# Gradient tail of an attention and MLP kernel: b2's sums and one addend of dx moved from products to VectorE, dx rows in two parts, other buffers

## The chip, the cores and the metric

The kernel runs on one core of a Trainium2 chip. A core has five engines, each with its own in-order queue: TensorE (PE, matrix products into PSUM; its weight loads are the row PEld), VectorE (DVE), ScalarE (ACT), GpSimd (POOL) and SyncE (SP, which here only issues transfers). Transfers issued by SP and POOL run on the core's 16 DMA engines. The metric is the device time of one execution in microseconds; a profile of one more execution shows what each engine did.

## The reference, cut to what matters

The forward function normalizes x, runs 32-head attention s on it, runs a gated MLP on it that has a second layer norm, and returns x + s * silu(MLP). What is computed is that output (out_0) and the gradients of a given grad_out for x, wqkv, wo, w1, b1, w2 and b2 (out_1 to out_7).

```python
xn = _layernorm(x, axis=-1)
s = _A_ref(xn, A_wqkv, A_wo)                     # softmax attention, H = 32, then @ wo
# _B_ref: y = _layernorm(xn); h = gelu(y @ w1 + b1); m = h @ w2 + b2
g = _silu(_B_ref(xn, B_w1, B_b1, B_w2, B_b2))
return x + s * g
# reference: _out, _vjp = jax.vjp(_f, A_x, A_wqkv, A_wo, B_w1, B_b1, B_w2, B_b2)
#            returns (_out, *_vjp(grad_out))
```

Sizes: S = 2048 rows, D = 512 columns, F = 1792 hidden units; all inputs and outputs bf16.

## The kernel before, in words

Rows are worked in NT = 16 tiles of 128, D in IC = 4 blocks of 128, F in FC = 14. Three parts follow each other. `Pre` normalizes, projects and runs the MLP forward (0 to about 220 us). `attention_core` runs the attention forward and backward for all heads (to about 1862 us). `Grads` computes the rest: its `tail_open` and `tail_mid` are called at the end of the attention loop, its `run` after it. The instructions of each engine run in the order in which the code emits them, and a step waits for the data and buffers that it needs; nothing reorders them. So the order of the code, the number of buffers in a ring, and the order of SP's transfers set the time.

The stages of `Grads.run`, with the lines that matter:

- **Rows of the output (so).** For each row tile t, `emit_oT` transposes the attention output (L575, copied by ScalarE, L577) and `emit_so` multiplies with wo (L584). VectorE makes two tiles from that product: dm (L586, kept in `dm_all`) and t1 (L588, float32, in the ring "t13" of two buffers). POOL adds x to t1 (L597) and stores two rows at a time (L599, out_0). `load_s1` (L526) loads the operands, two row tiles at a time, into four buffers; the two last lie in `s1w`, whose columns 12 to 15 of 16 are free. `emit_dmT` transposes dm (L719, L720) and, for b2's gradient, which is the sum of dm over all rows, multiplies it with a column of ones (L721), 16 products into one PSUM bank of its own (`psdb2`). From t = 12 on, dwo (L732) is mixed in.
- **dw2** (L742): 14 groups of 16 products. Each needs a transposed load of the hidden layer (`load_hg`, L711, four buffers). VectorE and ScalarE meanwhile compute the slope of gelu in 49 steps (`slope_step`, L667 to L688).
- **dwq, dwkv** (L822, L830): 12 groups of 16 products. SP's queue here holds, in this order of the loop index i: transposed loads of dKV (L793), of w2 (L790, two for each i from 4 to 10), of y (L860), and of w1 (L863, one for each i from 8 to 11).
- **dh and dy** by groups of four row tiles: `emit_dh` (L878) multiplies with w2T, VectorE multiplies each product with the slope and sums it for b1 (L881); the result goes out through transposes (L885, L886). `emit_dy` (L912) multiplies with w1T, and `ln_a` (L901 to L905) does the backward of a layer norm: ScalarE sums the row (L901), VectorE multiplies and sums (L902), combines (L904) and makes the bias (L905); ScalarE scales the row (L915, into `dxm_all`).
- **dw1** (L984): per four hidden blocks (`ci`) two passes of 32 products, over pieces that SP loads (L950) into five buffers; evictions in `evac` (ScalarE L727, VectorE L725), stores by POOL and SP (L993) from three output buffers.
- **dx rows** (L1013 to L1025), between the third and the fourth dw1: 13 products for each row tile, the first of them the identity times `dxm_all` (L1013), the share of the second layer norm; then `ln_a` on the PSUM result, ScalarE's scaling (L1020), the addition of grad_out on POOL (L1022, on VectorE for the two last), and the store (L1025). Operands come in groups of four row tiles by `load_dx` (L1003 to L1005).

The product tiles come from the PSUM ring `psA` (five banks), transposes from `psT` (two), and `psS` holds `psdb2`.

Of the kernel before, what the change touches and what calls it, by code (L numbers as in the profile page):

```python
# [489 lines left out]
class Grads:  # L490
# [88 lines left out]
    def emit_so(self, t):  # L579
        nc = self.nc  # L580
        oT = self.oTs.pop(t)
        ps = self.pA([128, D], f32, "ps_so")
        for cc in range(IC):
            nc.tensor.matmul(ps[:], lhsT=oT[:, cc, :], rhs=self.wo_sb[:, cc, :], start=(cc == 0), stop=(cc == IC - 1))  # L584
        g, x = self.s1[t // 2]
        nc.vector.tensor_tensor(out=self.dm_all[:, t, :], in0=ps[:], in1=g[:, t % 2, 1, :], op=ALU.mult)  # L586
        t1 = self.row("t13")
        nc.vector.tensor_tensor(out=t1[:], in0=ps[:], in1=g[:, t % 2, 0, :], op=ALU.mult)  # L588
        self.flush_adds()
        self.adds.append((t, t1, x))  # L590

    def flush_adds(self):
        nc = self.nc
        for t, t1, x in self.adds:
            if t % 2 == 0:
                self.ot = self.row("ot")
            nc.gpsimd.tensor_tensor(out=self.ot[:, t % 2, :], in0=t1[:], in1=x[:, t % 2, :], op=ALU.add)  # L597
# [12 lines left out]
    def run(self):  # L610
        nc, k, tc, ctx = self.nc, self.k, self.tc, self.ctx
        out_2, out_3, out_4, out_5, out_6, out_7 = self.outs[2:]
        slots = ctx.enter_context(tc.tile_pool(name="p3_slots", bufs=1, reuse_waits="tile"))
        psA = ctx.enter_context(tc.tile_pool(name="p3_psA", bufs=5, space=PSUM, reuse_waits="tile"))
        psS = ctx.enter_context(tc.tile_pool(name="p3_psS", bufs=1, space=PSUM, reuse_waits="tile"))
        psT = ctx.enter_context(tc.tile_pool(name="p3_psT", bufs=2, space=PSUM, reuse_waits="tile"))
        self.pT = lambda shape, dt, name: psT.tile(shape, dt, name=name, tag="tp")
        self.pA = lambda shape, dt, name: psA.tile(shape, dt, name=name, tag="mm")
# [14 lines left out]
        db1acc = slot("db1acc", [128, FC, 4], "db1acc", f32)  # L633
        db1f = slot("db1f", [128, FC], "db1f", f32)
        lns = [slot(f"lns{i}", [128, 4], f"lns{i}", f32) for i in range(4)]
        ones_bf = slot("ones", [128, 1], "ones_bf")
        db2 = slot("db2", [1, D], "db2")
        slot("pad", [128, 32], "pad_to_256g")
        self.s1w = slot("w2T", [128, NT, D], "s1w")
        sl = slot("sl", [128, 5, 4, 512], "sl")  # L640
# [70 lines left out]
            tr(out=hgr[:, fc % 4], in_=k.HGT_s[fc * 128:fc * 128 + 128, :])  # L711

        dmT, dm_all = self.dmT, self.dm_all
        psdb2 = psS.tile([1, D], f32, name="psdb2")

        def emit_dmT(t):
            pt = self.pT([128, IC, 128], bf16, "dm_tp")
            for b in range(IC):
                nc.tensor.transpose(pt[:, b, :], dm_all[:, t, b * 128:(b + 1) * 128], k.ident_bf[:])  # L719
            nc.scalar.copy(out=dmT[:, :, t * 128:(t + 1) * 128], in_=pt[:])  # L720
            nc.tensor.matmul(psdb2[0:1, :], lhsT=ones_bf[:, 0:1], rhs=dm_all[:, t, :], start=(t == 0), stop=(t == NT - 1))  # L721

        def evac(out, in_, e):
            if e:
# [25 lines left out]
        self.load_s1(3)  # L750
        self.load_s1(4)
        ld(out=dso_all[:, 0:8], in_=dsov[:, 0:8])
        nc.vector.memset(ones_bf[:], 1.0)

        nd = 0
        for t in range(2, NT):
# [22 lines left out]
        while nd < NT:  # L779
            emit_dmT(nd)  # L780
            nd += 1
        nc.vector.tensor_copy(out=db2[:], in_=psdb2[0:1, :])
        st(out=out_7.rearrange("(o d) -> o d", o=1), in_=db2[:])

        xn1 = slot("xg", [128, NT, D], "xn1")
        dKVn = [self.pO.tile([128, NT, 4, 128], bf16, name="dKVn0", tag="Oall")]
# [54 lines left out]
        for i in range(12):  # L841
            part, ic = i // 4, i % 4
            if part == 0:
                emit_dwq(ic)
            else:
                emit_dwkv(ic, part - 1)
            if i == 0:
                load_dkv(0, 3)
            if i < 3:
                load_h1(3, 1 + i)  # L850
            if 1 <= i <= 4:
                load_dkv(1, i - 1)
            if 4 <= i <= 10:
                for _ in range(2):
                    if nw < FC:
                        load_w2T(nw)
                        nw += 1
            if i == 7:
                y_all = self.pO.tile([128, NT, D], bf16, name="y_all", tag="Oall")
                ld(out=y_all[:], in_=k.Y_s.rearrange("(t p) d -> p t d", p=128))  # L860
            if i >= 8:
                j = i - 8
                tr(out=w1T[:, :, j, :], in_=self.B_w1[j * 128:j * 128 + 128, :])  # L863
            slope_step(1 + i % 2)


# [90 lines left out]
        for h4 in range(4):  # L957
            tr(out=dQT[:, 4 * h4:4 * h4 + 4].rearrange("c t b s -> c (t b) s"),
               in_=k.dQall[:, 4 * h4:4 * h4 + 4, :].rearrange("s t c -> s (t c)"))
        dy_group(2)  # L960
        R = [self.early.tile([128, 4, S], bf16, name="R0", tag="dmT"), None]
        rv = k.dKVT_s.rearrange("(r p) s -> p r s", p=128)
        dy_group(3)
        R[1] = slot("xg", [128, 4, S], "R1")
        xn_all = self.pO.tile([128, NT, D], bf16, name="xn_all", tag="dQall")
        dor = slot("hgw", [128, 3, 4, D], "dor")
        r2r = slot("gp1", [128, 4, D], "r2r", f32)
        dxr = slot("gp2", [128, 8, D], "dxr")
        nc.vector.reduce_sum(out=db1f[:], in_=db1acc[:], axis=AX.X)

# [2 lines left out]
        def emit_dw1(ci):  # L973
            c0, cn = CH[ci]
            w = cn * 128
            for ih in range(2):
                pss = [self.pA([128, 512], f32, "ps_dw1") for _ in range(2)]
                for tg in range(4):
                    pc = pieces[(ci, tg)]
                    for t4 in range(4):  # L980
                        t = tg * 4 + t4
                        for i2 in range(2):
                            ic = ih * 2 + i2
                            nc.tensor.matmul(pss[i2][:, 0:w], lhsT=y_all[:, t, ic * 128:(ic + 1) * 128], rhs=pc[:, 0:cn, t4, :],  # L984
                                             start=(t == 0), stop=(t == NT - 1))
                    if ih == 1 and nx[0] < 16:
                        pieces[order[nx[0]]] = load_piece(*order[nx[0]])
                        nx[0] += 1
                for i2 in range(2):
                    ic = ih * 2 + i2  # L990
                    ob = ob_tile()
                    evac(ob[:, 0:w], pss[i2][:, 0:w], i2)
                    (st if i2 and ci < 3 else ld)(out=out_4[ic * 128:(ic + 1) * 128, c0 * 128:c0 * 128 + w], in_=ob[:, 0:w])  # L993

        emit_dw1(0)
        psb = self.pT([FC, 128], f32, "db_tp")
        nc.tensor.transpose(psb[:], db1f[:], k.ident_f[:])
        db1 = slot("db2", [FC, 128], "db1")
# [9 lines left out]
        load_dx(0)  # L1008
        emit_dw1(2)
        load_dx(1)  # L1010
        for t in range(NT):
            ps = self.pA([128, D], f32, "ps_dxa")
            nc.tensor.matmul(ps[:], lhsT=k.ident_bf[:], rhs=dxm_all[:, t, :], start=True, stop=False)  # L1013
            for cc in range(IC):
                nc.tensor.matmul(ps[:], lhsT=dQT[:, t, cc, :], rhs=wT[:, cc, :, :], start=False, stop=False)
            for rc in range(8):
                nc.tensor.matmul(ps[:], lhsT=R[rc // 4][:, rc % 4, t * 128:(t + 1) * 128], rhs=wT[:, 4 + rc, :, :], start=False, stop=(rc == 7))
            r, nb = ln_a(ps[:], xn_all[:, t, :], k.rstd1[:, t:t + 1])
            r2 = r2r[:, t % 4, :]
            nc.scalar.activation(out=r2, in_=r[:], func=ACT.Identity, bias=nb, scale=k.rstd1[:, t:t + 1])  # L1020
            dx = dxr[:, t % 8, :]
# [1 line left out]
            if t in (1, 5):  # L1023
                load_dx(2 + t // 4)
            ld(out=self.o1[t * 128:(t + 1) * 128, :], in_=dx)  # L1025
        emit_dw1(3)


# [489 lines left out]
```

## Time and profile before

| what | us |
|---|---|
| median of 3 runs | 2208.2 (2205.89 to 2212.59) |
| profiled execution | 2206.27 |
| its span, first to last instruction | 2204.4 |
| PE busy in the span | 2147.6 (97%) |
| DVE busy | 1899.9 (86%) |
| ACT busy | 1758.4 (80%) |
| POOL busy | 590.3 (27%) |
| TensorE clock granted, mean | 0.998 |

The page and the trace give, for each line of the code, the busy time of its instructions, the idle time of the engine before them and what ended that idle time ("<- DVE dm_all L586"). A group is named by line, engine, operation and by what it writes and reads. Times in a timeline are from the start of the span. A busy PE is not a PE at its peak, and the idle time of an engine that nobody waits for costs nothing. Where an instruction waits for several things, the profile names the one that came last by its own record, which can be another than the true one.

### The profile page before, as it was taken

Reading aid. Unit: us, or ns where it says so; the run is one execution under the profiler, and the core shown is the slowest. Engines: PE = TensorE matmul, PEld = TensorE weight load, DVE = VectorE, ACT = ScalarE, POOL = GpSimd, SP = SyncE. Lnnn points to the kernel's source line nnn. Section 1 sums busy time; section 2 is a strip of 40 time slices with the busy share of each in tenths; the row PEclk is TensorE's granted clock in tenths of the full one; section 3 lists DMA queues with packets and bytes.
Section 4 is the critical chain, followed back from the end, with each engine's and each line's share of the span. In section 5 each row is a group of like instructions: output and inputs, shape, how many; then the busy total and the mean of one; then the engine's idle time right before and its main releaser. Section 6 shows DMA issues by size and latency. Waiting matters only on the chain.

```text
span 2204.4 us, 74272 instructions
## 1 busy us (share of the span) xinstructions
PE 2147.6 (97%) x30690; PEld 1192.5 (54%) x30690; DVE 1899.9 (86%) x3696; ACT 1758.4 (80%) x2481; POOL 590.3 (27%) x1373
## 2 busy tenths in 40 slices
PE   6999999999999999999999999999999999999998
PEld 3444555555555555555555555555555555444444
DVE  6677899999999999999999999999999998798624
ACT  5764888888888888988888989888888887784214
POOL 4276222122223222221312222222222132510002
PEclk9999999999999999999999999999999999999999
DMA  7786999999999999999999999999999999999974
GB/s 236 244 276 201 214 190 202 198 196 204 202 194 197 205 199 198 200 199 203 199 199 203 199 196 206 191 205 198 193 212 200 197 209 210 296 262 234 246 200 154
DMA packets 1422066, 461.14 MB, mean 209 GB/s; under 512 B 1334622, under 2 KB 1405918, under 8 KB 1421728
## 3 DMA queue, kind: packets, MB, share of 16 engines
q1 hardware_dynamic: 1407424, 425.46, 101.6%
q0 software_dynamic: 12720, 29.37, 4.9%
q8 instruction: 240, 3.93, 0.8%
q10 hardware_dynamic: 1584, 1.57, 0.2%
q14 instruction: 98, 0.80, 0.1%
HBM read 62.79 MB, written 64.75 MB: 58 GB/s over the span
## 4 chain that ended last, share of the span: by engine, by line
PE 90%; DVE 4%; issue 2%; ACT 2%; DMA 2%; POOL 1%; SPq 0%; DVEq 0%; ACTq 0%; POOLq 0%
PE tT L1194 24%; PE d L1115 15%; PE X L1229 10%; PE Z L1332 10%; PE X L1232 5%; PE X L1236 5%; PE ps_dw L742 2%; PE ps_dy L912 2%; PE ps_dw L984 2%; PE ps_h L352 2%; PE s L1093 2%; PE ps_m L367 2%; PE ps_dh L878 2%; PE tT L1264 1%; PE ps_dwkv L830 1%
## 5 line engine op out<-in xcount | busy, mean ns | idle before, releaser
L1133 DVE TENSOR_TENSOR gts<-d,ets 128x512 bf16<-128x512 f32 x2048 | 1366.4, 683 | 110.4 <-ACT ek L1211 46.7
L1102 ACT ACTIVATE ets<-s 128x1024 bf16<-128x1024 f32 x1024 | 1047.8, 1023 | 170.1 <-PE s L1093 82.2
L1194 PEld LDWEIGHTS <-ets 128*128 128x128 bf16 x6790 | 429.4, 97 | 248.3 <-issue 245.6
L1194 PE MATMUL tT<-ident_bf,ets 128*128 128x128 bf16 x6790 | 545.9, 219 | 14.2 <-ACT ek L1211 2.1
L1211 ACT COPY ek<-tT 128x448 f32<-128x448 f32 (+2 forms) x1024 | 510.4, 498 | 4.0 <-DVE ek L1211 1.3
L1115 PE MATMUL d<-QDT,KVT 32*128 32x512 bf16 x2048 | 450.0, 385 | 0.0
L1093 PE MATMUL s<-QDT,KVT 32*128 32x512 bf16 x2048 | 400.6, 381 | 2.6 <-ACT ets L1102 2.6
L1115 PEld LDWEIGHTS <-KVT 32*128 32x128 bf16 x2048 | 130.1, 91 | 319.2 <-issue 319.2
L1229 PE MATMUL X<-ets,NAT 128*32 128x256 bf16 x4096 | 300.5, 284 | 0.3 <-DVE xs L1245 0.3
L1236 PE MATMUL X<-gts,NAT 128*17 128x256 bf16 x4096 | 289.5, 273 | 0.0
L1232 PE MATMUL X<-ets,Lc 128*32 128x256 bf16 x4096 | 289.5, 273 | 0.0
L1392 POOL COPY tick<-gts 1x2 bf16<-1x2 bf16 x205 | 35.8, 174 | 629.7 <-DVE gts L1133 629.7
L1332 PE MATMUL Z<-gk,W 128*32 128x512 bf16 x2048 | 197.8, 379 | 1.1 <-DVE acc L1346 1.1
L1332 PE MATMUL Z<-ek,W 128*32 128x512 bf16 x1792 | 198.4, 379 | 0.0
L1229 PEld LDWEIGHTS <-NAT 128*32 128x32 bf16 x4096 | 105.9, 93 | 114.8 <-issue 21.9
L1293 POOL TENSOR_TENSOR W<-NATQq,rL 128x128 bf16<-128x128 bf16 x64 | 25.3, 396 | 503.4 <-DVE rL L1292 391.2
L1093 PEld LDWEIGHTS <-KVT 32*128 32x128 bf16 x2048 | 123.6, 91 | 8.5 <-issue 6.1
L1332 PEld LDWEIGHTS <-W 128*32 128x32 bf16 x4096 | 113.8, 97 | 11.7 <-issue 1.7
L1232 PEld LDWEIGHTS <-Lc 128*32 128x32 bf16 x4096 | 107.9, 96 | 0.0
L1236 PEld LDWEIGHTS <-NAT 128*17 128x17 bf16 x4096 | 103.4, 92 | 3.1
L1332 PE MATMUL Z<-ekd,W 128*32 128x512 bf16 x256 | 97.0, 379 | 0.0
L1197 PE MATMUL tT<-ident_bf,ets 128*128 128x128 bf16 x378 | 82.8, 219 | 0.0
(252 smaller groups left out, 2493.9 us busy)
## 6 DMA issues: line engine op xcount, KB each, us to landing
gk<-gts SPq DMA_TRANSPOSE x512, 5.3
H1T_s<-h1r SPq DMA_DIRECT2D x28, 256.0 KB, 3.9
HGT_s<-hgT SPq DMA_DIRECT2D x8, 896.0 KB, 4.4
DH_s<-stg SPq DMA_DIRECT2D x12, 512.0 KB, 3.2
hch<-DH_s SPq DMA_DIRECT2D x12, 512.0 KB, 4.4
gp<-H1T_s SPq DMA_DIRECT2D x9, 512.0 KB, 7.5
out_dram<-ob_w POOLq DMA_DIRECT2D x36, 128.0 KB, 4.6
NAT_s<-NS SPq DMA_DIRECT2D x4, 1056.0 KB, 6.2
```

The costliest lines, as they stand in the source:

```text
L352: nc.tensor.matmul(ps[:], lhsT=w1_sb[:, ic, fc * 128:(fc + 1) * 128], rhs=yT[:, ic, g * 512:(g + 1) * 512], start=(ic == 0), stop=(ic == I ...
L1093: nc.tensor.matmul(s[:, hj, :], lhsT=op["KVT"][r:r + 32, kb * 128:(kb + 1) * 128], rhs=op["QDT"][r:r + 32, qc * 512:(qc + 1) * 512], start ...
L1102: nc.scalar.activation(out=st_et[g][:, :, :, a[1] % 4, :].rearrange("k b h q -> k h b q"), in_=cur["s"][:].rearrange("k h (b q) -> k h b q ...
L1115: nc.tensor.matmul(d[:], lhsT=op["KVT"][r:r + 32, kb * 128:(kb + 1) * 128], rhs=op["QDT"][r:r + 32, qc * 512:(qc + 1) * 512], start=True, ...
L1133: nc.vector.tensor_tensor(out=gts[:, kb % 2, hj, :].rearrange("k (b q) -> k b q", b=4), in0=st_d.pop((g, hj))[:].rearrange("k (b q) -> k b ...
L1194: nc.tensor.transpose(tb[:, i - cut(g), :], et[:, b // 2, b % 2, kk, :], ident_bf[:])
L1197: nc.tensor.transpose(tb[:, 7, :], st_et[g // 16 * 16 + kk2][:, b // 2, b % 2, kk2, :], ident_bf[:])
L1211: copy(out=blk[j]["Ek"][kb // 4][:, kb % 4, lo:hi].rearrange("q i k -> q (i k)").bitcast(f32), in_=st_T[g][:, (lo - c) * 64:(hi - c) * 64])
L1229: nc.tensor.matmul(X[r:r + 32, 0:256], lhsT=NATt[:, kb, hj, 1:33], rhs=ev, start=(kb == 0), stop=False, skip_group_check=True, tile_positi ...
L1232: nc.tensor.matmul(X[r:r + 32, 256:512], lhsT=Lc[:], rhs=ev, start=False, stop=False, skip_group_check=True, tile_position=(0, r))
L1236: nc.tensor.matmul(X[r:r + 17, 256:512], lhsT=NATt[:, kb, hj, 0:17], rhs=gv, start=False, stop=(kb == 15), skip_group_check=True, tile_pos ...
L1332: nc.tensor.matmul(Z[r:r + 32, :], lhsT=WT[j % 2][1 - part][:, qb, hj, :], rhs=mv, start=(part == 0 and qb == 0), stop=(part == 1 and qb = ...
```

## The change

- b2's gradient is no longer summed by products. The 16 products and their PSUM bank go; the ring `psA` has six banks. After `dy_group(2)`, VectorE sums the four blocks of `dmT` along the rows (four reductions of 128 x 2048), and after the first dw1 a transpose turns the four columns into the stored row.
- t1 of every third and fourth row tile of four goes to the free columns of `s1w`, so that t1 has four buffers.
- w1's four transposed loads are issued together at i = 11, after all of w2's.
- In the dx rows, the identity product goes. VectorE adds `dxm_all` to the PSUM result and writes float32 into one of three buffers in SBUF (in the tile of `r2r`), and `ln_a` reads that. The scaling, the addition and the store of a row (`dx_out`) are emitted after the next row's products and `ln_a` (`dx_row`).
- In the last dw1, the two evictions of a pass go into one output buffer and leave in one store.

```diff
...
             nc.tensor.matmul(ps[:], lhsT=oT[:, cc, :], rhs=self.wo_sb[:, cc, :], start=(cc == 0), stop=(cc == IC - 1))
         g, x = self.s1[t // 2]
         nc.vector.tensor_tensor(out=self.dm_all[:, t, :], in0=ps[:], in1=g[:, t % 2, 1, :], op=ALU.mult)
-        t1 = self.row("t13")
-        nc.vector.tensor_tensor(out=t1[:], in0=ps[:], in1=g[:, t % 2, 0, :], op=ALU.mult)
+        if t % 4 < 2:
+            t1 = self.row("t13")[:]
+        else:
+            t1 = self.s1w[:, 8 + 2 * (t % 4):10 + 2 * (t % 4), :].rearrange("p x d -> p (x d)").bitcast(f32)
+        nc.vector.tensor_tensor(out=t1, in0=ps[:], in1=g[:, t % 2, 0, :], op=ALU.mult)
         self.flush_adds()
         self.adds.append((t, t1, x))
 
...
         nc, k, tc, ctx = self.nc, self.k, self.tc, self.ctx
         out_2, out_3, out_4, out_5, out_6, out_7 = self.outs[2:]
         slots = ctx.enter_context(tc.tile_pool(name="p3_slots", bufs=1, reuse_waits="tile"))
-        psA = ctx.enter_context(tc.tile_pool(name="p3_psA", bufs=5, space=PSUM, reuse_waits="tile"))
-        psS = ctx.enter_context(tc.tile_pool(name="p3_psS", bufs=1, space=PSUM, reuse_waits="tile"))
+        psA = ctx.enter_context(tc.tile_pool(name="p3_psA", bufs=6, space=PSUM, reuse_waits="tile"))
         psT = ctx.enter_context(tc.tile_pool(name="p3_psT", bufs=2, space=PSUM, reuse_waits="tile"))
         self.pT = lambda shape, dt, name: psT.tile(shape, dt, name=name, tag="tp")
         self.pA = lambda shape, dt, name: psA.tile(shape, dt, name=name, tag="mm")
...
         db1acc = slot("db1acc", [128, FC, 4], "db1acc", f32)
         db1f = slot("db1f", [128, FC], "db1f", f32)
         lns = [slot(f"lns{i}", [128, 4], f"lns{i}", f32) for i in range(4)]
-        ones_bf = slot("ones", [128, 1], "ones_bf")
-        db2 = slot("db2", [1, D], "db2")
+        db2c = slot("db2c", [128, IC], "db2c", f32)
+        slot("db2", [1, D], "db2")
         slot("pad", [128, 32], "pad_to_256g")
         self.s1w = slot("w2T", [128, NT, D], "s1w")
         sl = slot("sl", [128, 5, 4, 512], "sl")
...
             tr(out=hgr[:, fc % 4], in_=k.HGT_s[fc * 128:fc * 128 + 128, :])
 
         dmT, dm_all = self.dmT, self.dm_all
-        psdb2 = psS.tile([1, D], f32, name="psdb2")
 
         def emit_dmT(t):
             pt = self.pT([128, IC, 128], bf16, "dm_tp")
             for b in range(IC):
                 nc.tensor.transpose(pt[:, b, :], dm_all[:, t, b * 128:(b + 1) * 128], k.ident_bf[:])
             nc.scalar.copy(out=dmT[:, :, t * 128:(t + 1) * 128], in_=pt[:])
-            nc.tensor.matmul(psdb2[0:1, :], lhsT=ones_bf[:, 0:1], rhs=dm_all[:, t, :], start=(t == 0), stop=(t == NT - 1))
 
         def evac(out, in_, e):
             if e:
...
         while nd < NT:
             emit_dmT(nd)
             nd += 1
-        nc.vector.tensor_copy(out=db2[:], in_=psdb2[0:1, :])
-        st(out=out_7.rearrange("(o d) -> o d", o=1), in_=db2[:])
 
         xn1 = slot("xg", [128, NT, D], "xn1")
         dKVn = [self.pO.tile([128, NT, 4, 128], bf16, name="dKVn0", tag="Oall")]
...
             if i == 7:
                 y_all = self.pO.tile([128, NT, D], bf16, name="y_all", tag="Oall")
                 ld(out=y_all[:], in_=k.Y_s.rearrange("(t p) d -> p t d", p=128))
-            if i >= 8:
-                j = i - 8
-                tr(out=w1T[:, :, j, :], in_=self.B_w1[j * 128:j * 128 + 128, :])
+            if i == 11:
+                for j in range(IC):
+                    tr(out=w1T[:, :, j, :], in_=self.B_w1[j * 128:j * 128 + 128, :])
             slope_step(1 + i % 2)
 
 
...
             tr(out=dQT[:, 4 * h4:4 * h4 + 4].rearrange("c t b s -> c (t b) s"),
                in_=k.dQall[:, 4 * h4:4 * h4 + 4, :].rearrange("s t c -> s (t c)"))
         dy_group(2)
+        for ic in range(IC):
+            nc.vector.reduce_sum(out=db2c[:, ic:ic + 1], in_=dmT[:, ic, :], axis=AX.X)
         R = [self.early.tile([128, 4, S], bf16, name="R0", tag="dmT"), None]
         rv = k.dKVT_s.rearrange("(r p) s -> p r s", p=128)
         dy_group(3)
         R[1] = slot("xg", [128, 4, S], "R1")
         xn_all = self.pO.tile([128, NT, D], bf16, name="xn_all", tag="dQall")
         dor = slot("hgw", [128, 3, 4, D], "dor")
-        r2r = slot("gp1", [128, 4, D], "r2r", f32)
+        r2r = slot("gp1", [128, 7, D], "r2r", f32)
         dxr = slot("gp2", [128, 8, D], "dxr")
         nc.vector.reduce_sum(out=db1f[:], in_=db1acc[:], axis=AX.X)
 
...
                     if ih == 1 and nx[0] < 16:
                         pieces[order[nx[0]]] = load_piece(*order[nx[0]])
                         nx[0] += 1
+                if ci == 3:
+                    ob = ob_tile()
+                    for i2 in range(2):
+                        evac(ob[:, i2 * w:i2 * w + w], pss[i2][:, 0:w], i2)
+                    ld(out=out_4[ih * 256:(ih + 1) * 256, c0 * 128:c0 * 128 + w].rearrange("(x p) f -> p x f", p=128),
+                       in_=ob[:].rearrange("p (x f) -> p x f", x=2))
+                    continue
                 for i2 in range(2):
                     ic = ih * 2 + i2
                     ob = ob_tile()
                     evac(ob[:, 0:w], pss[i2][:, 0:w], i2)
-                    (st if i2 and ci < 3 else ld)(out=out_4[ic * 128:(ic + 1) * 128, c0 * 128:c0 * 128 + w], in_=ob[:, 0:w])
+                    (st if i2 else ld)(out=out_4[ic * 128:(ic + 1) * 128, c0 * 128:c0 * 128 + w], in_=ob[:, 0:w])
 
         emit_dw1(0)
+        psb2 = self.pT([IC, 128], f32, "db2_tp")
+        nc.tensor.transpose(psb2[:], db2c[:], k.ident_f[:])
+        db2 = slot("db2", [IC, 128], "db2")
+        nc.vector.tensor_copy(out=db2[:], in_=psb2[:])
+        st(out=out_7.rearrange("(c p) -> c p", p=128), in_=db2[:])
         psb = self.pT([FC, 128], f32, "db_tp")
         nc.tensor.transpose(psb[:], db1f[:], k.ident_f[:])
         db1 = slot("db2", [FC, 128], "db1")
...
         load_dx(0)
         emit_dw1(2)
         load_dx(1)
-        for t in range(NT):
+        def dx_row(t):
             ps = self.pA([128, D], f32, "ps_dxa")
-            nc.tensor.matmul(ps[:], lhsT=k.ident_bf[:], rhs=dxm_all[:, t, :], start=True, stop=False)
             for cc in range(IC):
-                nc.tensor.matmul(ps[:], lhsT=dQT[:, t, cc, :], rhs=wT[:, cc, :, :], start=False, stop=False)
+                nc.tensor.matmul(ps[:], lhsT=dQT[:, t, cc, :], rhs=wT[:, cc, :, :], start=(cc == 0), stop=False)
             for rc in range(8):
                 nc.tensor.matmul(ps[:], lhsT=R[rc // 4][:, rc % 4, t * 128:(t + 1) * 128], rhs=wT[:, 4 + rc, :, :], start=False, stop=(rc == 7))
-            r, nb = ln_a(ps[:], xn_all[:, t, :], k.rstd1[:, t:t + 1])
+            xa = r2r[:, 4 + t % 3, :]
+            nc.vector.tensor_tensor(out=xa, in0=ps[:], in1=dxm_all[:, t, :], op=ALU.add)
+            return ln_a(xa, xn_all[:, t, :], k.rstd1[:, t:t + 1])
+
+        def dx_out(t, r, nb):
             r2 = r2r[:, t % 4, :]
             nc.scalar.activation(out=r2, in_=r[:], func=ACT.Identity, bias=nb, scale=k.rstd1[:, t:t + 1])
             dx = dxr[:, t % 8, :]
...
             if t in (1, 5):
                 load_dx(2 + t // 4)
             ld(out=self.o1[t * 128:(t + 1) * 128, :], in_=dx)
+
+        prev = None
+        for t in range(NT):
+            row = dx_row(t)
+            if prev:
+                dx_out(t - 1, *prev)
+            prev = row
+        dx_out(NT - 1, *prev)
         emit_dw1(3)
 
 
...
```

More of the change, by code (lines that the diff above doesn't have):

```diff
@@ L596, in flush_adds @@
                 self.ot = self.row("ot")
-            nc.gpsimd.tensor_tensor(out=self.ot[:, t % 2, :], in0=t1[:], in1=x[:, t % 2, :], op=ALU.add)
+            nc.gpsimd.tensor_tensor(out=self.ot[:, t % 2, :], in0=t1, in1=x[:, t % 2, :], op=ALU.add)
             if t % 2 == 1:
@@ L752, in run @@
         ld(out=dso_all[:, 0:8], in_=dsov[:, 0:8])
-        nc.vector.memset(ones_bf[:], 1.0)
         nd = 0
```

## The prediction

> **What bounds the kernel now.** I read the busy times by stretch first, to find the stages after the attention loop (the change touches nothing before 1871 us), then the waits, then the stretch of each changed line in order of time. The tail runs from 1862 to 2204.4 us. Its stretches (us from : to, length, busy time and count by engine, granted clock, share of the 16 DMA engines, GB/s):
>
> ```profile
> 1866.00:1890.00 24.00, 21.37 (x195) 11.12 (x194) 14.32 (x25) 10.51 (x20) 17.42 (x24) 1.00 0.94 319
> 1890.00:1914.00 24.00, 23.07 (x128) 10.84 (x129) 16.15 (x20) 16.72 (x18) 11.97 (x14) 1.00 1.14 263
> 1914.00:1962.00 48.00, 47.32 (x220) 21.16 (x218) 45.88 (x53) 41.70 (x36) 10.77 (x17) 1.00 1.10 274
> 1962.00:1991.00 29.00, 28.81 (x134) 12.88 (x132) 26.21 (x32) 24.23 (x24) 4.97 (x8) 1.00 1.16 247
> ```
>
> PE looks like the bound everywhere (the first number after the length), but the last column but one says that from 1866 to 1991 the DMA engines are full too. PE's rare pauses there show which of the two sets the pace:
>
> ```profile
> 1959.56 3.63 PE L742 MATMUL ps_dw<-dm_all,hgr 128*128 128x512 bf16 x16 [0.66 <-ACT ob_w L727]
> 1991.69 8.58 PE L830 MATMUL ps_dwkv<-dKVn,xn 128*128 128x512 bf16 x39 [0.88 <-ACT ob_w L836]
> 2017.39 6.22 PE L878 MATMUL ps_dh<-dmT,w2T 128*128 128x512 bf16 x28 [1.36 <-DMA w2T<-in_B_w_dram]
> 2023.78 7.93 PE L878 MATMUL ps_dh<-dmT,w2T 128*128 128x512 bf16 x36 [0.17 <-DVE db1acc L881]
> ```
>
> The first two name ScalarE, but the transfer that the same instruction waits for landed at 1959.51 (the last hgr) and 1991.44 (the last dKVn): PE waits for data at all of the first three. From 2023.8 to 2190.5 PE does not pause.
>
> The last stage, the rows of dx, has another bound. One row and the end:
>
> ```profile
> 2179.61 0.57 ACT L901 ACTIVATE oT<-ps_dxa 128x512 bf16<-128x512 f32 x1
> 2180.31 0.69 DVE L902 CUSTOM_DVE_ANT_0 ot<-ps_dxa,xn_all 128x512 bf16<-128x512 f32 x1 [1.51 <-ACT oT L901]
> 2181.04 0.75 DVE L904 SCALAR_TENSOR_TENSOR t<-xn_all,lns,ps_dxa 128x512 f32<-128x512 bf16 x1
> 2181.71 0.21 DVE L905 TENSOR_SCALAR lns<-lns,rstd 128x1 f32<-128x1 f32 x1
> 2182.01 0.81 ACT L1020 ACTIVATE r2r<-t,lns,rstd 128x512 f32<-128x512 f32 x1 [1.74 <-DVE lns L905]
> 2182.73 0.57 ACT L901 ACTIVATE oT<-ps_dxa 128x512 bf16<-128x512 f32 x1
> ...
> 2190.51 7.36 PE L984 MATMUL ps_dw<-hch,y_all 128*128 128x256 bf16 x64
> ...
> 2201.36 0.42 DVE L725 CAST ob_w<-ps_dw 128x256 bf16<-128x256 f32 x1 [1.84 <-DMA out_dram<-ob_w]
> ```
>
> A row is a serial loop: ScalarE's sum (L901), VectorE's product (L902) that starts only after it, L904, L905, ScalarE's L1020, and only then the next row's L901: 2182.73 - 2179.61 = 3.12 us. PE needs 2.805 (starts of L1013 at 2184.90 and 2187.70), so the loop falls behind PE and ends with it by chance: PE's last product ends near 2197.7, the loop's L1020 at 2198.4, and then four evictions queue, the last for an output buffer, until 2204.4, 6.7 us after PE.
>
> **The change part by part.** The sum is against the profiled execution: 2206.27 us, span 2204.4, 1.87 around it, taken as unchanged. The median of the runs, 2208.2, lies 1.9 above it; I add that at the end.
>
> *b2's products go (L721).* 16 products at 0.31 us (starts 1874.35 to the next work at 1874.66, and so each time) are 5.0 us of PE. With t1 in four buffers VectorE's waits for POOL's additions in 1893 to 1913 (5.4 us at L588) shrink too. Neither shortens the kernel, I think: PE would reach the dw2 products near 1908.7 instead of 1913.64, but the fifth hgr landed at 1926.72, used at 1927.46, and the queue behind it is full (share 1.10). Ends: 0 and -5.0. I take 0, nearest to the pauses at 1959.56 and 1991.69, which sit on landings. The cover is the DMA queue; the additions that free the s1 buffers for SP's loads are themselves paced by out_dram's landings (1876.20 issued, 1883.04 landed, addition at 1883.17), so SP does not start earlier.
>
> *w1T's transposes behind w2T's.* SP issued w1T at 2005.74 (3.60 us), 2012.00, 2016.69, 2018.29, w2T in between, its last at 2015.38. Moved, two w1T issues (5.1 us) leave w2T's way, and it lands near 2013 where PE wants it at 2015.9: the 1.36 us pause goes. Next late is VectorE: its 15th L881 of this stage ended at 2023.72 and PE ran five buffers ahead; with six (the pool gains the bank of b2's sum) the tile that waits for it is one later, so PE saves one tile, four products of 0.216: -0.86 us. Ends -2.0 (no wait left) and 0. w1T keeps its place before the stg transposes (2020.42), landed by 2023.14, needed at 2030.7: 7 us of cover.
>
> *Four reductions on VectorE.* Nearest rows: 512 elements 676 ns (L266), 56 elements 202 ns (L969): 1.04 ns each, so 2048 take 2.27 us, four 9.1. They stand ahead of rows 12 to 15 in VectorE's queue, whose last ScalarE step moves from 2107.8 to about 2114.5 (after the 0.86 above). PE has six accumulators and does not notice. Behind them ScalarE's first dw1 eviction ends near 2115.1 instead of 2111.5, SP stores it and only then loads the next pieces: first load 2115.4 instead of 2112.89, landing 3.1 to 4.3 us later (2126.82 to 2129.93; 2114.62 to 2118.89), needed at 2119.1. Ends 0 and +0.7, taken +0.2. Their transpose costs PE as L997's: 0.11. The second copy into the same small tile waits for b2's store (4 us, as L1000's landing); VectorE's next work is at 2124, covered.
>
> *The dx rows.* PE loses one of 13 products: 16 x 0.216 = -3.45 us. VectorE gains an addition from PSUM (as L588: 0.69, with the handover 0.72); its row is 0.72 + 0.74 (L902 with its read) + 0.66 + 0.12 = 2.24 us, if L902 no longer waits for ScalarE. It waited, I read, because both read one PSUM bank: in the first MLP stage too, L356 never started before L354 had ended on the same tile, at least 33 ns after in all 56 pairs. Now both read an SBUF copy. L1020 comes after the next row's sum, so ScalarE's row is 0.67 + 0.72 = 1.39, outside the loop. POOL's addition is 1.15.
>
> Here a row speaks against the change. Two SBUF operands on VectorE and POOL's addition exclude each other:
>
> ```profile
> 1912.01 2.36 DVE L677 TENSOR_TENSOR sl<-sl,gp 128x2048 bf16<-128x2048 bf16 x1
> 1912.11 1.17 POOL L597 TENSOR_TENSOR ot<-t,s1w 128x512 bf16<-128x512 f32 x1
> ```
>
> L677 is 1.23 elsewhere; it was held by POOL's 1.17. L902 and L904 now read PSUM and one SBUF operand, and do not lengthen beside POOL (at most 692 and 749 ns); after the change both read SBUF twice. If all of POOL's time came on top, the row would be 3.39 us. But POOL starts 2.3 us into a row, when L904 is ending, and runs beside L905 and the next addition from PSUM, so the exclusive part is 1.15 + 0.74 + 0.75 = 2.64 us a row against PE's 2.589. I take 2.64: 0.8 us of lag over 16 rows, hidden under the 7.36 us of the last dw1.
> [...]
>
> *The end.* Nothing queues any more: the last eviction follows PE at once. 0.43 + 0.03 + 1.67 (landing of 128 KB, as dxr's) + 1.06 (2203.34 to the end) = 3.2 us after PE instead of 6.7: -3.5.
>
> Sum: -0.86 + 0.2 + 0.11 - 3.45 - 3.5 = -7.5. Span 2196.9, execution 2198.8, on the median's scale 2200.7 us. A measurement here can tell about 0.3%, 6.6 us, from no change (2201.6 and 2214.8).
>
> **Rivals.**
> 1. *PE's time of the b2 products reaches the end.* For it: PE is busy 97% of the span. Against: DMA share above 1.0 until 1991. -7.5 - 5.0 = -12.5: 2195.7.
> 2. *L902 keeps waiting for ScalarE's sum* (the two write columns of one small tile, lns). Row 0.72 + 0.70 + 1.52 (from L901's start to L902's; L902 to the next slot) = 2.94. The end after row starts is about T + 10.0 + 15 rows, T the start of the stage, now 2144.9 (the before: 2145.6): 2144.9 + 54.1 = 2199.0, -5.4: 2202.8. Against: the 33 ns pairs share only PSUM.
> 3. *POOL's addition comes wholly on top:* 3.39 a row, 2205.8, +1.4: 2209.6. For it: L677. Against: POOL's phase above.
> 4. *Slower: the row stays serial and only gets longer.* Place: the xa copies lie in one tile with r2r. If the buffers are not held apart, the addition of a row waits for L1020 and the loop is 3.12 + 0.72 = 3.84: 2212.5, +8.1: 2216.3. It decides from 3.30 us a row (break even), 3.74 for 0.3%. Against: slices of s1w were loaded (1885.45) while others of it were read.
>
> **How the numbers follow.** Forecast 0.60, rivals 0.12, 0.10, 0.05, 0.13 in order. The forecast's own range is 2198.5 to 2203.0 (the ends of the w1T part, the piece load, and the rows up to 2.85 us); 0.09 of its 0.60 lies short of 0.3%. Faster 0.51 + 0.12 = 0.63; same 0.09 + 0.10 + 0.05 = 0.24; slower 0.13. The range 2195.0 to 2210.0 takes in all but rival 4.
>
> **What would show it.** Right: L878 without a pause at w2T; PE still pausing in the dw2 products, now more, at hgr landings; the dh stage starting near 2005.5; rows of dx 2.6 us apart on VectorE with no L902 <- L901 wait; about 3 us from PE's last product to the end. Wrong: dh starting near 2000 (rival 1); L902 idle before each row (2); L902 or L904 near 1.8 us (3); the new addition waiting for L1020 (4); PE waiting for hch in the second dw1 (the reductions).

## The result

The changed kernel takes 2202.74 us (median of 13 runs, 2198.70 to 2208.50), the kernel before 2209.58 us (13 runs beside it): ratio 0.997, 95% interval 0.9959 to 0.998, so 6.84 us less (-9.1 to -4.4 by the interval). 7.5 less was forecast; the interval can't tell the two apart. In time the forecast, 2200.7, lies 2.0 under the measured one, and 1.4 of that is the kernel before: its median was 2208.2 in the three runs of the forecast and is 2209.58 in the 13 here.

The profiled execution took 2204.06 us, its span 2202.0. It can't be laid over the one of before as it stands: the first transpose of the output stage starts at 1862.38 us in the one and at 1865.16 in the other, although no code ahead of it differs, and over all profiled kernels of this study it starts between 1862.38 and 1870.68. This scatter is larger than the effect, so I read each stage from its own start. By the first products of the stages in the trace, from the output stage to dh it was 143.12 us and is 144.82, from dh to the dx rows 140.12 and 139.89, from there to the end of the span 58.83 and 52.12. The dx rows and the end carry the gain: -6.71. (All three together give -5.24 in these two executions, since the first stretch is 1.70 longer in the one of the changed kernel; how far that column scatters is said under the table below.) The stretches of the changed kernel, with the columns of those shown of before:

```profile
1866.00:1890.00 24.00, 21.86 (x223) 12.74 (x220) 16.24 (x27) 12.67 (x24) 16.44 (x26) 1.00 0.90 298
1890.00:1914.00 24.00, 20.78 (x110) 9.73 (x109) 16.51 (x20) 16.56 (x18) 14.35 (x16) 0.93 1.12 280
1914.00:1962.00 48.00, 44.71 (x201) 19.88 (x200) 42.99 (x48) 38.03 (x34) 10.38 (x16) 0.96 1.11 268
1962.00:1991.00 29.00, 29.00 (x136) 13.12 (x135) 25.56 (x30) 24.85 (x23) 4.93 (x8) 1.00 1.13 241
```

PE is busy 2.3 and 2.6 us less in the second and third stretch, the DMA share is as full as before, and the granted clock, 1.00 before, is 0.93 and 0.96: in each of the two PE runs at half its clock for 3.41 us. PE's pauses in the timeline:

```profile
1896.09 3.31 PE L732 MATMUL ps_dwo<-dso_all,Oall 128*128 128x512 bf16 x8 [2.04 <-DMA dso_all<-DSO_s]
1930.84 1.46 PE L742 MATMUL ps_dw<-dm_all,hgr 128*128 128x512 bf16 x3 [3.29 <-DMA hgr<-HGT_s]
1996.17 2.10 PE L827 MATMUL ps_dwkv<-dKVn,xn 128*128 128x512 bf16 x9 [1.49 <-DMA dKVn<-dKVT_s]
2028.26 7.07 PE L875 MATMUL ps_dh<-dmT,w2T 128*128 128x512 bf16 x32 [0.85 <-DVE db1acc L878]
2123.97 3.40 PE L983 MATMUL ps_dw<-hch,y_all 128*128 128x512 bf16 x15 [0.37 <-DMA hch<-DH_s]
```

The time of b2's products has become waiting for transfers (dso_all, hgr, dKVn); the pause at w2T is gone, VectorE is next there, and the pieces of dw1 come 0.37 late. One row of dx, and the end:

```profile
2168.93 0.69 DVE L899 CUSTOM_DVE_ANT_0 ot<-r2r,xn_all 128x512 bf16<-128x512 f32 x1
2168.99 0.63 ACT L898 ACTIVATE oT<-r2r 128x512 bf16<-128x512 f32 x1 [1.16 <-DVE r2r L1029]
2169.73 0.75 DVE L901 SCALAR_TENSOR_TENSOR t<-xn_all,lns,r2r 128x512 f32<-128x512 bf16 x1
2170.40 0.21 DVE L902 TENSOR_SCALAR lns<-lns,rstd 128x1 f32<-128x1 f32 x1
2170.49 1.16 POOL L1036 TENSOR_TENSOR dxr<-r2r,dor 128x512 bf16<-128x512 f32 x1 [1.44 <-ACT r2r L1034]
2171.52 0.69 DVE L899 CUSTOM_DVE_ANT_0 ot<-r2r,xn_all 128x512 bf16<-128x512 f32 x1
...
2191.31 7.15 PE L983 MATMUL ps_dw<-hch,y_all 128*128 128x256 bf16 x64
...
2198.50 0.42 DVE L725 CAST ob_w<-ps_dw 128x256 bf16<-128x256 f32 x1 [2.62 <-PE ps_dw L983]
```

L899 comes every 2.59 us, which is PE's 12 products; it no longer waits for ScalarE; POOL's addition starts beside L902, 2.3 us into the row as forecast, and ends 0.13 us after the next L899 has begun, which still takes its 0.69. The last eviction waits for PE alone; the span ends 3.53 us after PE's last product (6.57 before).

### The profile page after: what moved, and what is told of

Its sections match the earlier page's. It is cut to its first block, busy times and chain, and to the rows that moved or that the text cites. A ratio compares the mean times of both kernels' runs of the same rounds, so it can differ in the third digit from the quotient of the medians.

```text
span 2202.0 us, 74231 instructions
## 1 busy us (share of the span) xinstructions
PE 2143.2 (97%) x30659; PEld 1191.6 (54%) x30659; DVE 1921.1 (87%) x3715; ACT 1759.3 (80%) x2481; POOL 593.1 (27%) x1373
## 4 chain that ended last, share of the span: by engine, by line
PE 91%; DVE 3%; DMA 2%; ACT 1%; issue 1%; SPq 1%; POOL 0%; DVEq 0%; ACTq 0%; POOLq 0%
PE tT L1216 23%; PE d L1137 15%; PE X L1251 10%; PE Z L1354 10%; PE X L1254 5%; PE X L1258 5%; PE ps_dy L909 2%; PE ps_dw L983 2%; PE ps_dw L742 2%; PE s L1115 2%; PE ps_h L352 2%; PE ps_m L367 2%; PE ps_dh L875 2%; PE tT L1286 1%; PE ps_dxa L1027 1%; PE ps_qkv L210 1%
```

## The experiments

The times stand against runs of the kernel before on the same chip: ratio and 95% interval. The marks are read as above.

| kernel | ratio | output stage to dh | dh to dx | dx to end |
|---|---|---|---|---|
| before | 1 | 143.12 | 140.12 | 58.83 |
| changed | 0.997 (0.9959 to 0.998) | 144.82 | 139.89 | 52.12 |
| dx rows alone | 0.9958 (0.9944 to 0.9972) | 140.37 | 140.11 | 52.12 |
| b2 alone | 0.9999 (0.9988 to 1.0011) | 143.80 | 140.34 | 58.85 |
| changed, b2 by products | 0.9968 (0.9953 to 0.9982) | 142.14 | 140.12 | 52.12 |
| the same, sixth bank later | 0.9963 (0.9947 to 0.9979) | 143.93 | 139.25 | 52.12 |
| changed, filler products | 0.9971 (0.9958 to 0.9985) | 142.37 | 139.93 | 52.11 |
| changed, LN from PSUM | 0.9978 (0.9968 to 0.9988) | 144.67 | 140.02 | 55.58 |
| changed, rows in one part | 0.9988 (0.9973 to 1.0003) | 142.67 | 139.89 | 57.38 |
| the same, POOL's addition halved | one execution | 143.15 | 139.62 | 52.12 |
| changed, stores apart | 0.9946 (0.9928 to 0.9964) | 142.97 | 140.03 | 52.02 |
| fewer stores, b2 by products | 0.9944 (0.9929 to 0.996) | 138.54 | 140.11 | 52.12 |
| fewer stores, changed | 0.9925 (0.9908 to 0.9942) | 134.06 | 139.92 | 52.12 |

The last column repeats within 0.03 us between the kernels with the same code there, and the middle one within 0.15, but for "POOL's addition halved", which has 139.62 where its like have 139.89 to 140.03. The first column doesn't repeat: up to dh, before and "dx rows alone" are the same code and differ by 2.75.

**1. The dx rows alone.** The kernel before with the new rows, the larger r2r and the joined last stores; b2, w1's loads and t1 as before.

> The kernel before with the dx rows and the joined last store of the change, nothing else of it. Theory (rows bound by PE, end freed): all of the gain lies here, first dx row to the end of the span 52.1 us as with the whole change against 58.8 before, so -6.7 us, about 2202.9; the two halves of the tail ahead of it as before (first so transpose to dh 143.1 us). Rival 1 (the gain needs the sixth accumulator, because VectorE's addition holds the banks longer): first row to end above 53.5 us, -5 us or less. Rival 2 (part of the whole change's -6.8 came from the other parts): between -3 and -5 us.

52.12, as with the whole change, and the time falls by as much (0.9958 against 0.997, with intervals that overlap). The rows need neither the sixth accumulator nor the rest, and the times show no gain from the rest.

**2. b2 alone.** The kernel before with

```diff
-            nc.tensor.matmul(psdb2[0:1, :], lhsT=ones_bf[:, 0:1], rhs=dm_all[:, t, :], start=(t == 0), stop=(t == NT - 1))
...
         dy_group(2)
+        for ic in range(IC):
+            nc.vector.reduce_sum(out=db2c[:, ic:ic + 1], in_=dmT[:, ic, :], axis=AX.X)
```

the transpose and store of the change, and the bank given to psA.

> The kernel before with b2's sum by VectorE (the 16 products gone, four reductions, the pool with six accumulators), nothing else of the change. Theory of the clock: PE now comes to the dwo and dw2 products before their loads, pauses 2 us or more there, and runs at half its clock for about 3.4 us after each such pause; first so transpose to dh start about 144.8 us against 143.1 before, so +1 to +2 us in all (the sixth accumulator takes back up to 0.9). Rival 1, of the prediction (the transfers set the pace, nothing is gained or lost): 0 to -0.9. Rival 2 (the PE time reaches the end): -4 to -5 us.

Nothing gained, nothing lost: 0.9999, or -2.7 to +2.4 us. PE's waits in that stage (total, times, longest):

```profile
PE dm_tp L717 <- DVE dm_all L586: 5.7, 3, 2.6
PE ps_dwkv L824 <- DMA dKVn<-dKVT_s: 2.9, 1, 2.9
PE ps_dh L872 <- DMA w2T<-in_B_w_dram: 1.3, 1, 1.3
```

The 5 us are waited away again, first for VectorE (t1 still has two buffers), then for dKVn. Rival 2 falls. The time is too coarse to tell the clock's +1 to +2 from the prediction's 0.

**3. Products put back, and filler products.** One kernel is the changed one with b2's 16 products as before. The other is the changed one with products nobody reads, where PE had paused:

```diff
+        def filler(n):
+            pj = self.pT([128, D], f32, "filler")
+            for j in range(n):
+                nc.tensor.matmul(pj[:], lhsT=dm_all[:, 0, 0:128], rhs=dm_all[:, 0, :], start=(j == 0), stop=(j == n - 1))
...
             for t in range(NT):
+                if ac == 0 and t == 8:
+                    filler(9)
...
         for fc in range(FC):
+            if fc == 4:
+                filler(12)
             emit_dw2(fc)
```

> The changed kernel with b2's 16 products put back (and so five accumulators, no reductions, the separate small store of b2 as before); the rows of dx, w1's transposes behind w2's and t1 in four buffers stay. Theory of the clock: the products fill PE's pauses, no stretch at half clock between 1880 and 1965 us, first so transpose to dh near 143 us: 1.5 to 2 us faster than the changed kernel, about -8.5 us against before. Rival (transfers alone set that stage): within 0.5 us of the changed kernel, -6 to -7.5. If the products cost what they take on PE: 4 to 5 us slower than the changed kernel.

> The changed kernel with products whose result nothing reads put where PE paused: 9 in the middle of the first dwo product (1.9 us) and 12 ahead of the fifth dw2 product (2.6 us). They add only PE work. Theory of the clock: no pause over 1.4 us is left there, so no stretch at half clock, the next products run at 216 ns instead of 430, first so transpose to dh 143 to 143.5 us against 144.8: 1.3 to 1.8 us faster than the changed kernel although PE has 4.5 us more to do. Rival 1 (the transfers set the pace and the slow clock is hidden behind them): the same time within 0.5 us. Rival 2 (the added products delay PE): 1 to 4.5 us slower.

In both, PE's longest wait between 1862 and 2030 us is 1.2 and 1.3 us (3.3 in the changed kernel), the mean granted clock of the profiled execution is 0.997 and 0.998 (0.996), and 4.5 to 5 us of additional PE work cost nothing: dh starts at 142.14 and 142.37. That is what the clock theory asked for. But over all kernels with all stores the column does not part by that mean clock: "LN from PSUM" has 144.67 at 0.998, "the same, sixth bank later" 143.93 at 0.998, "dx rows alone" 140.37 at 0.997, "rows in one part" 142.67 at 0.997. And before and "dx rows alone", the same code up to dh, with longest waits of 1.4 and 1.5 us and mean clocks of 0.998 and 0.997, differ by 2.75; the long pauses ahead of the changed kernel's slow stretches (2.04 and 3.29 us) lengthen the column too. In the times both kernels are level with the changed one, but intervals of 6 us can't tell the 1.3 to 2 us that were expected. So the price of the slow clock over this stage is not shown; that the products are free there is, by both columns and by experiment 2.

**4. The cover taken away.** If full DMA queues hide b2's products, fewer transfers must bring the products to light. Both kernels leave out the stores of dw2's 14 output tiles (128 KB each) and the first 7 of out_0's 8 (256 KB each), 21 stores and 3.7 MB (the expectations below say 22 and 5.6 MB, which was miscounted); the condition on fc is never met:

```diff
-            st(out=out_6[fc * 128:(fc + 1) * 128, :], in_=ob[:])
+            if fc == 15:
+                st(out=out_6[fc * 128:(fc + 1) * 128, :], in_=ob[:])
...
-            if t % 2 == 1:
+            if t == 15:
                 nc.gpsimd.dma_start(out=self.o0.rearrange("(t p) d -> p t d", p=128)[:, t - 1:t + 1], in_=self.ot[:])
```

> The changed kernel with b2's products put back, and 22 of the stores of the stage left out: dw2's first 15 output tiles (128 KB each) and out_0's first 7 (512 KB each) are computed and not stored, so 5.6 MB less go through the queues between 1880 and 1990 us and those outputs are wrong. Read against the next run, which has the same stores left out and no products. If the transfers are what covers b2's products, this kernel pays for them once the transfers are fewer: first so transpose to dh about 4 to 5 us later than in the next run. It is also itself earlier there than with all stores (142.1 us), to 135 or less.

> The changed kernel with the same 22 stores left out. Theory (the transfers cover the products): first so transpose to dh 4 to 5 us less than in the run with the products, and no pause of PE over 2 us there. Rival (what paces the stage is not the volume but the order, VectorE's and POOL's steps and SP's queue of transposing loads): both at the same time within 1.5 us, and pauses at dso_all and hgr as with all stores.

138.54 with the products (135 or less was expected), 134.06 without: 4.48 us, by the marks of a stage in which neither kernel pauses for long. By the times it is less: the medians of four runs each, 2196.65 and 2193.38, are 3.3 us apart, and the slowest run of the one (2194.29) is faster than the fastest of the other (2194.78). So the products cost 3 to 4.5 us here. With the products, PE waits for no transfer at all; without them this is left:

```profile
PE ps_dwo L732 <- DMA dso_all<-DSO_s: 0.9, 1, 0.9
PE ps_dh L876 <- DVE db1acc L879: 0.8, 1, 0.8
```

With all stores the same edit gained nothing. So the cover lies with the transfers. Whether it is their volume is not shown: with the stores POOL's issuing of them goes too, and the landings that the buffers of `ot` and `ob_w` wait for. The share of the DMA engines does not tell it either. From 1914 to 1962 us the two kernels have, with the products and without:

```profile
1914.00:1962.00 48.00, 47.74 (x219) 21.73 (x223) 45.77 (x53) 40.28 (x37) 3.48 (x4) 1.00 0.98 230
1914.00:1962.00 48.00, 47.74 (x219) 21.75 (x223) 45.67 (x52) 41.78 (x38) 2.48 (x3) 1.00 1.04 249
```

The shares, 0.98 and 1.04, are close to the 1.10 of before, and yet PE hardly waits here. The prediction took a share about 1 as the sign that PE's time is covered; PE's waits, and a run with fewer transfers, are better ones.

**5. The LN from PSUM.** The changed kernel with the identity product back and `ln_a(ps[:], ...)`, still in two parts:

```diff
-            xa = r2r[:, 4 + t % 3, :]
-            nc.vector.tensor_tensor(out=xa, in0=ps[:], in1=dxm_all[:, t, :], op=ALU.add)
-            return ln_a(xa, xn_all[:, t, :], k.rstd1[:, t:t + 1])
+            return ln_a(ps[:], xn_all[:, t, :], k.rstd1[:, t:t + 1])
```

> The changed kernel with dx's rows summed on PE again (the identity product back, 13 products a row) and the LN reading PSUM, but still in two parts. Theory (two parts alone break the loop, since ScalarE's sum no longer waits for the row's own last step): VectorE's product waits for ScalarE's sum again (both read the bank), a row is 0.70 + 1.52 = 2.22 us on VectorE, PE's 2.805 is the bound; first dx row to the end 52.1 + 16 x 0.216 = 55.6 us, 3.2 us less than before. Rival (the loop stays, ScalarE's L1034 of the row ahead holds the sum back): about 2.94 a row, 58 us or more, within 1 us of before.

55.58, as the theory said. A row in the timeline:

```profile
2174.95 0.60 ACT L898 ACTIVATE oT<-ps_dxa 128x512 bf16<-128x512 f32 x1 [1.41 <-PE ps_dxa L1028]
2175.45 0.20 ACT L898 ACTIVATION_READ_ACCUMULATOR oT<-ps_dxa 128x1 f32 x1
2175.68 0.69 DVE L899 CUSTOM_DVE_ANT_0 ot<-ps_dxa,xn_all 128x512 bf16<-128x512 f32 x1 [1.20 <-ACT oT L898]
```

VectorE's product waits for ScalarE's sum on the bank, 0.03 us after it, as before the change. With an SBUF copy it starts 0.06 us ahead of the sum. But the sum itself now waits for PE, not for the row ahead: the two parts break the loop (58.83 to 55.58, -3.25), and taking the product off PE gives the rest (55.58 to 52.12, -3.46). The sixth accumulator and the joined store are in the -3.25 too; experiments 1 and 7 reach 52.12 and 52.02 without the one or the other.

**6. Rows in one part.** The changed kernel with

```diff
-        prev = None
         for t in range(NT):
-            row = dx_row(t)
-            if prev:
-                dx_out(t - 1, *prev)
-            prev = row
-        dx_out(NT - 1, *prev)
+            dx_out(t, *dx_row(t))
```

> The changed kernel with each row's last part right behind its first, so that POOL's addition starts about 1 us into the next row instead of 2.4 us, beside VectorE's two instructions with two SBUF operands (0.69 and 0.75 us). Theory A (these two exclude POOL's 1.16 us, as the 2.36 us addition of the prediction showed): one of them takes about 1.8 us, a row 2.3 to 3.4 us by how much overlaps; if all of it comes on top, 3.4 a row and first dx row to end 65 us, 6 us slower than before. Theory B (no exclusion between these, the earlier case had another cause): the durations stay 0.69 and 0.75, the row stays at PE's 2.59, first dx row to end 52.1 to 52.6, same time as the changed kernel.

Theory A: 57.38, of the 6.71 only 1.45 is left.

```profile
2174.24 0.69 DVE L899 CUSTOM_DVE_ANT_0 ot<-r2r,xn_all 128x512 bf16<-128x512 f32 x1
...
2174.60 1.35 POOL L1036 TENSOR_TENSOR dxr<-r2r,dor 128x512 bf16<-128x512 f32 x1 [1.66 <-ACT r2r L1034]
...
2174.98 1.52 DVE L901 SCALAR_TENSOR_TENSOR t<-xn_all,lns,r2r 128x512 f32<-128x512 bf16 x1
```

POOL starts beside L899 and takes 1.35 instead of 1.16; L901, behind it, takes 1.52 instead of 0.75 and ends 0.55 after POOL. The row is 3.01. In this row the instruction that starts second is the one that gets longer: POOL's addition, 0.36 us into L899's 0.69, by 0.19, and L901, 0.38 us into POOL's 1.35, by 0.77.

To tell POOL from ScalarE as the cause, POOL's addition was halved: in the same kernel rows 0 to 13 add and store 256 of the 512 columns.

```diff
+            hw = D if t >= 14 else D // 2
-            (V if t >= 14 else nc.gpsimd).tensor_tensor(out=dx, in0=r2, in1=dor[:, (t // 4) % 3, t % 4, :], op=ALU.add)
+            (V if t >= 14 else nc.gpsimd).tensor_tensor(out=dx[:, 0:hw], in0=r2[:, 0:hw], in1=dor[:, (t // 4) % 3, t % 4, 0:hw], op=ALU.add)
```

> The kernel with the rows not in two parts, and POOL's addition (and the store) of rows 0 to 13 on 256 of the 512 columns, so that half of out_1's rows is left out. With all columns L901 took 1.52 us and ended 0.55 us after POOL's addition of 1.35. If POOL's addition is what holds L901, then half of it (about 0.6 us) frees L901 about 0.6 us sooner: L901 0.75 to 0.95 us, a row at PE's 2.59 and first dx row to end about 52 to 54 us against 57.4. If something else of the order holds L901 (ScalarE's sum reading the same tile, or the wait for the accumulator's read), it stays at 1.5 and the row at 3.0.

```profile
2168.49 0.93 POOL L1037 TENSOR_TENSOR dxr<-r2r,dor 128x256 bf16<-128x256 f32 x1 [1.66 <-ACT r2r L1034]
...
2168.93 1.03 DVE L901 SCALAR_TENSOR_TENSOR t<-xn_all,lns,r2r 128x512 f32<-128x512 bf16 x1
```

L901 falls to 1.03, again ending 0.54 after POOL; the row is back at PE's 2.59 and the stage at 52.12. POOL is the cause. (L901 is a little above the 0.95 expected; POOL, too, takes longer than the 0.6 estimated, 0.93.)

**7. The last stores apart.** The changed kernel with the last dw1's four stores as before.

> The changed kernel with the last four stores of dw1 apart again, as before. Theory (the end is free because the rows no longer delay the evictions, and the third and first output buffers are free in time): first dx row to the end within 0.3 us of 52.1. Rival (the joined store carries a part of it, because the last eviction waits for an output buffer): 53.3 to 54 us, 1.2 to 1.8 us slower.

52.02: the joined store gives nothing. (The ratio, 0.9946 from four runs, is the lowest of all kernels with all stores; its interval overlaps with that of the changed kernel, and none of the columns shows a gain that would go with it.)

**8. All that helped, together.** The changed kernel with b2 by products, whose bank becomes the sixth accumulator once the sum is read:

```diff
+            if self.six and self.np % 6 == 0:
+                return psS.tile(shape, dt, name=name, tag="six")
             return psA.tile(shape, dt, name=name, tag="mm")
...
         st(out=out_7.rearrange("(o d) -> o d", o=1), in_=db2[:])
+        self.six, self.np = True, 0
```

> The changed kernel with b2's sum by products as before, and the bank of that sum as sixth accumulator once the sum is read. Theory: no reductions and no second small transpose, so no wait for hch in the second dw1 (0.37) and no 0.11; the sixth accumulator and w1's transposes behind w2's give 0.7: dh start to first dx row 139.4 to 139.5 us (140.1 before, 139.9 changed), first dx row to end 52.1; about -7.5 us against before, 0.5 to 1 better than the changed kernel, less than can be told from the times. Rival (the sixth accumulator gives nothing without the rest): 140.1 as with five.

dh to dx 139.25, against 140.12 with five accumulators and w1's loads moved alike: the sixth gives 0.87, and w1's loads behind w2's give 0.00 without it. Against the changed kernel 0.64 is won, the price of the reductions: 0.11 for the transpose, and the rest at the pause for hch. That pause costs more than the 0.37 us that its row shows as idle: in the changed kernel the eight products ahead of it start at 2121.72 and the next at 2123.97, 2.25 us, where eight products take 1.73 (0.216 each), so 0.52 is lost. The pause is not the same in each execution: in "POOL's addition halved", with the same reductions, the trace shows no wait for hch, and dh to dx is 139.62. In time the kernel is level with the changed kernel, as are all kernels with 52.12 and all stores.

## Why the prediction was right, point by point

- *b2's products, 0.* Right, and in the way given: experiment 2 gains nothing, PE waits for dso_all, hgr and dKVn instead, and experiment 4 brings out 3 to 4.5 of the 5.0 us once 21 stores are left out. Rival 1 is refuted for the kernel with all its stores. The sign that it went by, a DMA share above 1.0, does not tell the two cases apart (experiment 4), and it missed the two stretches of 3.41 us at half clock that came with PE's pauses of 2.04 and 3.29 us.
- *w1's loads and the sixth accumulator, -0.86.* Measured -0.87 (experiment 8). From dh's first product to dy's it is 26.05 us before, 26.06 with w1's loads moved alone (b2 by products), 25.62 with the sixth accumulator alone (b2 alone) and 25.18 with both (changed). So the order alone gives nothing, since VectorE stands right behind w2T; the accumulator alone gives 0.43.
- *The reductions and their transpose, +0.31.* Measured 0.64. The reductions took 2.28 us each (2.27 estimated), the transpose its 0.11; the pause for hch cost 0.52 where 0.2 was taken (inside 0 to 0.7). The 0.64 and the 0.43 of the sixth accumulator also give "b2 alone": 0.21 more from dh to dx than before, and 140.34 against 140.12 is 0.22.
- *The dx rows, -3.45.* Measured -3.46. VectorE's row was put at 2.24; it is 2.41, still under PE's 2.59. The 2.64 taken as the exclusive part, and so the 0.8 us of lag, did not come: when L899 starts, 0.13 us are left of POOL's addition, and no instruction of the row takes longer for it. Where it starts 1.2 us earlier in the row, the row is 3.01 (experiment 6).
- *The end, -3.5.* Measured -3.25. The span ends 3.53 us after PE's last product instead of 6.57, which is -3.04 (3.2 instead of 6.7 was forecast); the other -0.21 is the last dw1, 7.15 us instead of 7.36, which the forecast did not have. The joined store has no part in it.
- *Rival 2* (L902 keeps waiting, 2.94 a row) had its price wrong: in experiment 5 the wait is there and the row is still PE's 2.805, since the sum no longer waits for the row ahead. The formula for the ends of the rivals, T + 10.0 + 15 rows, was about 2 us low: for "rows in one part" (T 2146.86, rows of 3.01) it gives 2202.0, and the span is 2204.2. *Rival 3* was a matter of phase, not of the operands alone. *Rival 4* did not come: no addition waited for L1034.
- The dh stage was expected 143.1 us after the output stage's start; it came at 144.82. Kernels without b2's products (full stores, no filler) have 142.67 to 144.82, with them 140.37 to 143.93. Whether dropping the products costs some 1 us there, and whether by the half clock (experiment 3), stays open.

So 7.5 was 0.3 too much at the reductions and 0.25 at the end: 6.94 by the two settled columns, 6.84 by the times. That these two agree to 0.1 is more than the times can tell.

## What to carry to other kernels

Work taken off PE became waiting here in the stage whose DMA share was 0.94 to 1.16: 5.0 us of products less, and a ratio of 0.9999. So look at what the pauses sit on before counting such work. In the dx rows, which run through several engines, emitting a row's last part behind the next row's first broke the loop and at the same time chose beside which VectorE instruction POOL runs; both were needed here (3.25 us from the loop, 5.26 lost without the split once the operands lie in SBUF). Of two parts aimed at the same waits, one can be worth nothing alone and the other half: w1's loads 0.00, the sixth accumulator 0.43, both 0.87.

## What the runs showed of the hardware

PE's granted clock fell with some pauses of over 2 us and not with others. In the changed kernel two stretches of 3.41 us at half clock begin at 1896.39 and 1930.52, 34.13 us apart, ten times their own length; from 1899.80 to 1930.52 and from 1933.93 to 2198 the mean granted clock is 1.00. The first begins 0.30 us after PE has gone on from its pause of 2.04 us, the second while PE still stands in its pause of 3.29. In the 3.41 us ahead of them PE was idle for 2.04 and 2.98 us, 60% and 87%. If the trace is cut into pieces of that length from the first point on, both ways, no other piece from 1862 to 2197 us has more than 1.18 us idle, and the two slow ones are the only ones below full clock. In the kernel before, whose longest pause there is 1.36 us, the mean clock from 1860 to 2198 us is 1.00.

"b2 alone" has three pauses of over 2.5 us. With the one of 2.61 us that ends at 1896.38, ten products of dwo take 3.81 us, where at 0.216 apart they would take 2.32. With the one of 2.90 us that ends at 1994.85, fifteen products of dwkv take 3.40, which is the 0.216 apart, and with the one of 2.58 that ends at 1887.65 the next four products of L584 take their 1.03 as before it. So a length of pause alone did not tell what the clock did.

In the changed kernel's slow stretches the products start 0.427 us apart, elsewhere 0.216, so that eight of them, 3.41 us, cost 1.69 us more. The same 1.69 us stand between two rows of the profile, "LN from PSUM" first, with its pause of 2.63 us, and then the changed kernel, whose clock is 1.00 there:

```profile
1993.92 15.66 PE L827 MATMUL ps_dwkv<-dKVn,xn 128*128 128x512 bf16 x64 [2.63 <-ACT gp3a L683]
1996.17 13.97 PE L827 MATMUL ps_dwkv<-dKVn,xn 128*128 128x512 bf16 x64 [1.49 <-DMA dKVn<-dKVT_s]
```

From the first of these 64 products to dh's first it is 15.50 us against 13.81. No wait follows ahead of dh, and the 1.69 us are not taken back from dh to the dx rows (140.02 against 139.89). Where PE next waits for a transfer, as after both stretches of the changed kernel (hgr 3.29 us, dKVn 1.49 us), the loss can be taken back there, and how much of it is stays open.
